# Two Fourier heads on one core: x of the second head in rotating tiles, its stores without an order among themselves, six compare buffers and a narrower rank-one product

## The chip, the cores and the metric

The kernel runs on one core of a Trainium2 chip. The time is that of one execution in device microseconds, lower is better; the figure is the median of several executions. A profile is one further execution, recorded by the hardware profiler.

## What is computed

Two independent heads, each on a tensor of 2048 rows by 512 columns in float32, written side by side. Head A is a global filter (a 2D real FFT, a product with a complex weight, the inverse). Head B is FNet mixing: two DFT matrices come in as inputs, and the real part of the double transform goes out.

```python
def _A_ref(x, w_r, w_i):
    X = jnp.fft.rfft2(x, axes=(-2, -1))
    return jnp.fft.irfft2(X * (w_r + 1j * w_i), s=(S, D), axes=(-2, -1))

def _B_ref(x, dft_seq_re, dft_seq_im, dft_hid_re, dft_hid_im):
    a = jnp.einsum("bsd,ed->bse", x, dft_hid_re)
    b = jnp.einsum("bsd,ed->bse", x, dft_hid_im)
    return jnp.einsum("ts,bse->bte", dft_seq_re, a) - jnp.einsum("ts,bse->bte", dft_seq_im, b)

return jnp.concatenate([A, B], axis=-1)
```

## The kernel before

The kernel does not multiply by B's matrices. It computes both heads by fast transforms with its own small tables, and beside that it reads B's matrices completely (36 MB) and checks that they are the DFT matrices which the fast way assumes. The sum of all differences gives a flag; if it is not small, a slow general way (`_b_from_c`) runs after the branch. With the usual inputs only the branch is paid. So three streams of work share the engines:

*The compare stream* (`compare`, `compare_hidden`). 64 pieces of 512 KB of the sequence matrices and 4 of the hidden ones are loaded by SP to buffers named `raw` (three, the constant RAW), VectorE (DVE) forms the difference with a table piece `tt` (lines L309 and L311), and ScalarE (ACT) sums the absolute values of two pieces at once (L302). The pieces come in a fixed order; C_AT pins each to a step of A's work, so that it is not done before it.

*Head A* (`a_work`). `forward` loads x of A to `zv`, adds and subtracts halves on DVE, and for eight pairs of groups does the transform along the hidden dimension (L455, 128x256, into PSUM, copied by ACT L489), then the first step along the sequence (L455, 128x512, copied by L496). POOL stores the result to `out_a` as a bounce buffer (16 stores, L498), and SP loads it back in another layout to `zv` (eight loads, L510). Eight slots follow (`slot`): DVE sums (L226), a product with the `ft` table, the weight product on DVE, sums on DVE, two-column corrections on POOL (L581, L582), a product with the `it` table, and a copy back into `zv` by ACT (L600). When all eight are done, `inverse` runs 256 products on TensorE (PE) in two halves (from `zv`, then from `sda`) with copies by ACT (L619, L630), and SP stores `out_a` (L634).

*Head B* (`b_work`). `b_load` brings x of B to a region `big` by eight loads of 512 KB and one small one, and POOL copies its middle column (L373). Each load fills 64 partitions: a half of the partitions holds four groups of rows, the other half the mirrored rows in reverse. Four folds on DVE (`b_fold`, even part to a `yb` tile, odd part in place), 64 products along the sequence (`b_along`, L397, copied by ACT L401 to L403), nine steps along the hidden dimension (`b_hidden`, L410 to L415; L412 is a rank-one product of one row with 257 columns of a table that is zero in every second one), and eight output row groups (`b_rows`): a product (L422 and its kin), a copy to a row buffer `yb` (L429; two buffers, YB), two sums on DVE, a mirrored copy (L432), a direct store (L440, L442) and an indirect one that scatters the mirrored rows (L443), both on POOL's queue. All these stores write the tensor `out_b`, and the framework orders each behind the ones before it.

What sets the order: B_AT names the step of A after which each step of B is issued, C_AT pins the compares; a scheduler of the framework then places the instructions of every engine in one fixed sequence and puts in the semaphore waits. An engine, POOL's and SP's queues too, works strictly in that sequence: an instruction that waits holds up all behind it. Each DMA also waits for the DMA issued eight before it on its queue, since eight semaphores go round.

Of the kernel before, what the change touches and what calls it, by code (L numbers as in the profile page):

```python
# [10 lines left out]
F32 = mybir.dt.float32  # L11
# [55 lines left out]
def _tables_b():  # L67
# [133 lines left out]
def kernel(  # L201
# [43 lines left out]
    def region(name):  # L245

        return ap.tile([P, 8208 if name == "big" else 8192], F32, name=name)
# [12 lines left out]
    hc = bp.tile([P, 2, 257], F32, name="hc")  # L260
# [101 lines left out]
    def b_load():  # L362

        xt = region("big")
        x = xt.rearrange("p (g d) -> p g d", g=16)
        src = xb.rearrange("b a d -> (b a) d")
# [7 lines left out]
        nc.gpsimd.dma_start(fb, tabs["fb"].rearrange("p k (j s) -> p k j s", j=8))  # L374
        nc.sync.dma_start(hc, tabs["hc"])
        hidden_table()
        nc.sync.dma_start(mb, tabs["mb"])
        return x

    def b_fold(q, x):  # L380

        v = x[:, 4 * q : 4 * q + 4]
        ev = bp.tile([P, 2, 512], F32, name="yb", bufs=YB).rearrange("p k (g d) -> p (k g) d", g=2)
        TT(out=ev, in0=v[:, :, :256], in1=v[:, :, 512:256:-1], op=ADD)
        TT(out=v[:, :, :256], in0=v[:, :, :256], in1=v[:, :, 512:256:-1], op=SUB)
# [19 lines left out]
    def b_hidden(e, zb):  # L405
# [4 lines left out]
        nc.tensor.matmul(out, ye[:, :, 0, at[0]], hc[:, 0], start=True, stop=False)  # L410
        nc.tensor.matmul(out, ye[:, :, 1, at[0]], ht[:, 1, 0], start=False, stop=False)
        nc.tensor.matmul(out, yo[0:1, :, at[1]], hc[0:1, 1], start=False, stop=True)  # L412
        for c in range(2):
            nc.tensor.matmul(bank[:, 257:], yo[:, :, at[2] + 16 * c], ht[:, c, 1, 1:256], start=c == 0, stop=c == 1)  # L414
        nc.scalar.copy(zb[:, e], bank)  # L415

    def b_rows(o, zb):
# [16 lines left out]
        if o == 0:  # L434
            bank = ps_b.tile([P, 512], F32, name="pb")
            nc.tensor.matmul(bank[0:1, :257], mb[:, 1408:], zb[:, 0, :257], start=True, stop=True)
            nc.scalar.copy(y[0:1, 1, :257], bank[0:1, :257])
            nc.scalar.copy(y[0:1, 1, 257:], y[0:1, 1, 255:0:-1])
            for k in range(2):
                nc.gpsimd.dma_start(rows[8 * k, :64], y[64 * k : 64 * k + 64, 0])  # L440
        else:
            nc.gpsimd.dma_start(rows[o], y[:, 0])  # L442
# [389 lines left out]
```

## Time and profile before

| | us |
|---|---|
| median of 3 runs | 277.77 |
| lowest, highest | 274.91, 278.9 |
| the profiled execution | 278.1 |
| its span, first to last instruction | 276.3 |

| engine | busy us | share of the span |
|---|---|---|
| PE (matmuls) | 211.5 | 77% |
| DVE | 161.2 | 58% |
| ACT | 136.0 | 49% |
| POOL | 42.8 | 15% |

The DMA engines moved 73.85 MB at a mean of 267 GB/s. No engine is busy throughout, so the shares alone do not say what sets the time; it has to be read stage by stage. In the rows of the profile, "out<-in" names the tiles written and read, "xN" is a count, and the bracket at the end gives the idle time ahead of an instruction on its engine and what ended it. "SPq" and "POOLq" are the engines as issuers of DMAs. A row of the waits reads: engine and line, what it waited for, us in total, how often, the longest. "PEclk" is the share of full clock that TensorE was granted. A row of 128x256 or so of PE often counts each product as two matmul records.

### The profile page before, as it was taken

The numbers are of one execution on the slowest core, as the hardware profiler recorded it, in microseconds if no ns is written. First come the engines' busy times: TensorE is split into PE (matmuls) and PEld (weight loads), VectorE is DVE, ScalarE is ACT, GpSimd is POOL, SyncE is SP. The second block draws the span as 40 slices with busy tenths as digits, with TensorE's granted clock in tenths as the row PEclk, the third lists the DMA queues.
The fourth block names the chain that finished last, engine by engine and source line by source line (L and its number), as shares of the span: only waits on it lengthen the run. The fifth ranks groups of instructions, "written<-read, shape, count | busy, mean of one in ns | idle before, by whom it ended". The sixth has DMA issues, their size and how long they took to land.

```text
span 276.3 us, 2713 instructions
## 1 busy us (share of the span) xinstructions
PE 211.5 (77%) x833; PEld 169.0 (61%) x833; DVE 161.2 (58%) x225; ACT 136.0 (49%) x219; POOL 42.8 (15%) x80
## 2 busy tenths in 40 slices
PE   5049999299878799999999676302999995999630
PEld 1039788177678358787875445002799994876520
DVE  0860001685748359797968679745485754675340
ACT  1001430649866251856337235415678775774570
POOL 3000120013210016250213333013010100000000
PEclk9658999899955599999999797755599999899795
DMA  7999999889995998585844343775979888889763
GB/s 256 403 243 214 215 379 418 293 267 343 354 401 181 367 399 311 193 248 194 289 145 109 141 161 103 288 250 208 284 250 332 298 259 294 273 279 369 287 264 126
DMA packets 27460, 73.85 MB, mean 267 GB/s; under 512 B 2928, under 2 KB 9072, under 8 KB 26928
## 3 DMA queue, kind: packets, MB, share of 16 engines
q1 hardware_dynamic: 24432, 64.48, 70.5%
q0 software_dynamic: 2720, 8.56, 8.2%
q10 hardware_dynamic: 288, 0.59, 0.7%
q8 instruction: 8, 0.13, 0.2%
q14 instruction: 12, 0.10, 0.1%
HBM read 61.03 MB, written 12.58 MB: 266 GB/s over the span
## 4 chain that ended last, share of the span: by engine, by line
DMA 48%; PE 24%; DVE 13%; issue 8%; ACT 4%; SPq 1%; POOL 0%; DVEq 0%; POOLq 0%; ACTq 0%
DMA raw<-in_cm 23%; PE pa L455 12%; DMA ht<-tab_ht 6%; DMA out_b<-yb,turn 6%; DMA big<-in_xb 6%; DVE ec L309 5%; PE pb L414 4%; DVE ec L311 3%; PE pb L412 3%; DMA zv<-in_xa 2%; DMA zv<-out_a 2%; ACT ec L302 2%; DMA out_b<-yb 2%; DVE yb L226 2%; DVE sda L226 2%
## 5 line engine op out<-in xcount | busy, mean ns | idle before, releaser
L302 ACT ACTIVATE ec<-ec 128x2048 bf16<-128x2048 bf16 x34 | 65.0, 1911 | 33.4 <-DVE ec L311 21.8
L311 DVE TENSOR_TENSOR ec<-raw,tt 128x512 bf16<-128x512 f32 (+1 forms) x48 | 40.0, 865 | 51.7 <-DMA raw<-in_cm 51.6
L309 DVE SCALAR_TENSOR_TENSOR ec<-tt,odd,raw 128x512 bf16<-128x512 f32 (+1 forms) x48 | 42.5, 926 | 19.2 <-DMA raw<-in_cm 18.9
L455 PE MATMUL pa<-zb,sda 128*128 128x256 f32 x128 | 32.2, 410 | 12.2 <-DVE sda L226 12.2
L455 PEld LDWEIGHTS pa<-zb,sda 128*128 128x128 f32 x128 | 30.4, 307 | 15.5 <-DVE sda L226 13.1
L455 PE MATMUL pa<-ye,sda 128*128 128x256 f32 x128 | 32.2, 414 | 6.5 <-ACT zb L630 3.4
L455 PEld LDWEIGHTS pa<-ye,sda 128*128 128x128 f32 x128 | 26.4, 208 | 12.2 <-ACT zb L630 4.6
L455 PE MATMUL pa<-it,sda 128*128 128x128 f32 x112 | 19.2, 339 | 17.9 <-POOL sda L581 16.0
L455 PEld LDWEIGHTS pa<-it,sda 128*128 128x128 f32 x112 | 17.9, 246 | 23.6 <-POOL sda L581 20.1
L455 PE MATMUL pa<-ye,zv 128*128 128x256 f32 x128 | 30.5, 403 | 0.7 <-ACT zv L600 0.7
L455 PEld LDWEIGHTS pa<-ye,zv 128*128 128x128 f32 x128 | 29.3, 306 | 1.8 <-ACT zv L600 1.0
L226 DVE TENSOR_TENSOR sda<-zv 128x512 f32<-128x512 f32 x30 | 19.5, 687 | 15.4 <-DMA zv<-in_xa 7.5
L226 DVE TENSOR_TENSOR sda<-sda 128x512 f32<-128x512 f32 (+1 forms) x34 | 23.0, 717 | 0.3
L489 ACT COPY zb<-pa 128x1024 f32<-128x1024 f32 x8 | 8.1, 1007 | 28.5 <-PE pa L455 28.5
L226 DVE TENSOR_TENSOR sda<-pa,sda 128x1024 f32<-128x1024 f32 (+1 forms) x16 | 17.7, 1151 | 5.6 <-ACT sda L557 3.9
L455 PE MATMUL pa<-zb 128*128 128x512 f32 x32 | 16.6, 645 | 5.5 <-ACT zb L489 5.5
L397 PE MATMUL pb<-fb,yb 128*128 128x72 f32 x64 | 14.5, 319 | 3.1 <-ACT ye L403 3.1
L397 PEld LDWEIGHTS pb<-fb,yb 128*128 128x128 f32 x64 | 13.1, 248 | 6.2 <-ACT ye L403 4.0
L397 PE MATMUL pb<-fb,big 128*128 128x128 f32 (+1 forms) x64 | 16.5, 351 | 0.0
L498 POOL DMA_DIRECT2D out_a<-zb x16 | 8.5, 534 | 49.5 <-ACT zb L496 49.3
L429 ACT COPY yb<-pb 128x514 f32<-128x514 f32 x8 | 4.7, 587 | 19.4 <-DMA out_b<-yb,turn 17.1
L397 PEld LDWEIGHTS pb<-fb,big 128*128 128x128 f32 x64 | 13.1, 251 | 1.0 <-issue 1.0
(78 smaller groups left out, 247.0 us busy)
## 6 DMA issues: line engine op xcount, KB each, us to landing
raw<-in_cm SPq DMA_DIRECT2D x64, 512.0 KB, 4.9
tt<-tab_tt SPq DMA_DIRECT2D x8, 513.0 KB, 10.3
zv<-in_xa SPq DMA_DIRECT2D x8, 512.0 KB, 8.6
big<-in_xb SPq DMA_DIRECT2D x8, 512.0 KB, 16.1
out_a<-zb POOLq DMA_DIRECT2D x16, 256.0 KB, 6.2
sda<-in_wa SPq DMA_DIRECT2D x16, 256.0 KB, 3.4
zv<-out_a SPq DMA_DIRECT2D x8, 512.0 KB, 8.7
out_a<-zb SPq DMA_DIRECT2D x4, 1024.0 KB, 6.9
```

What stands on the lines that cost most here:

```text
L226: last[0] = nc.vector.tensor_tensor(**kw)
L302: nc.scalar.activation(flat, flat, mybir.ActivationFunctionType.Abs, accum_out=stat[:, i : i + 1])
L309: nc.vector.scalar_tensor_tensor(out, v, odd[:, k : k + 1], raw, op0=MUL, op1=SUB)
L311: nc.vector.tensor_tensor(out=out, in0=raw, in1=v, op=ADD if flip else SUB)
L397: nc.tensor.matmul(bank[:, at : at + n].rearrange("p (j s) -> p j s", j=8), v[:, cols], f[:, :, k], start=True, stop=True)
L412: nc.tensor.matmul(out, yo[0:1, :, at[1]], hc[0:1, 1], start=False, stop=True)
L414: nc.tensor.matmul(bank[:, 257:], yo[:, :, at[2] + 16 * c], ht[:, c, 1, 1:256], start=c == 0, stop=c == 1)
L429: nc.scalar.copy(y[:, :, :257], bank[:, :257].unsqueeze(1).to_broadcast([P, 2, 257]))
L455: mma[0] = nc.tensor.matmul(*args, **kw)
L489: nc.scalar.copy(zs[p], pd[p])
L498: nc.gpsimd.dma_start(bounce[:, 2 * p + k], ys[:, k])
```

## The change

It has five parts and new numbers in both tables.

- x of B is loaded to tiles `xq` (two, of 128 partitions by four groups), each by four loads of 256 KB to all 128 partitions (partition 2r holds row r of a group, partition 2r+1 its mirror); the first two quarters at the start, the third and fourth after the first and second have been used. The table `fb` is permuted to match. POOL's copy of the middle column is gone: each fold is now two instructions of 4 x 255 columns and two of 4 columns instead of two of 1024. The region `big` is gone, and the nine results of `b_hidden` lie in the two `xq` buffers and a tile of their own.
- The stores of `out_b` are declared independent of each other.
- RAW is 6 instead of 3.
- The rank-one product reads a tile of ones and writes 128 columns, every second one of the output; the table `hc` loses its second half.
- B_AT and C_AT are new.

```diff
-RAW = 3
-B_AT = [4, 10, 10, 12, 12, 14, 14, 14, 14, 15, ..., 26, 28, 30, 32, 35, 38, 40, 42]
+RAW = 6
+B_AT = [2, 6, 6, 8, 8, 8, 8, 8, 8, 8, 8, 8, 11, 12, 17, 19, 19, 19, 19, 26, 28, 30, 32, 35, 38, 38, 42]
...
-        for q in range(4):
-            g = slice(4 * q, 4 * q + 4)
-            for half, lo in enumerate((1 + 16 * q, 112 - 16 * q)):
-                v = src[16 * lo : 16 * lo + 256].rearrange("(g r) d -> r g d", g=4)
-                load(x[64 * half : 64 * half + 64, g, :512], v[:, ::-1] if half else v)
-        load(x[64:80, 15, :512], src[:16])
-        nc.gpsimd.tensor_copy(x[:, :, 512], x[:, :, 256])
...
+    def b_load(q):
+        x = bp.tile([P, 4, 512], F32, name="xq", bufs=2)
+        for k in range(4):
+            g = 4 * q + k
+            lo, hi = 1 + 4 * g, 124 - 4 * g
+            load(x[:, k], bass.AP(xb.tensor, xb.offset + 16 * D * lo, [[D, 64], [16 * D * (hi - lo), 2], [1, D]]))
+        if q == 3:
+            load(x[1:32:2, 3], xb[0])
+        return x
...
-        TT(out=ev, in0=v[:, :, :256], in1=v[:, :, 512:256:-1], op=ADD)
-        TT(out=v[:, :, :256], in0=v[:, :, :256], in1=v[:, :, 512:256:-1], op=SUB)
+        for out, op in ((ev, ADD), (x, SUB)):
+            TT(out=out[:, :, 1:256], in0=x[:, :, 1:256], in1=x[:, :, 511:256:-1], op=op)
+            TT(out=out[:, :, 0], in0=x[:, :, 0], in1=x[:, :, 256], op=op)
...
-        nc.tensor.matmul(out, yo[0:1, :, at[1]], hc[0:1, 1], start=False, stop=True)
+        nc.tensor.matmul(bank[:, 1:257:2], yo[0:1, :, at[1]], ones[0:1], start=False, stop=True)
...
+        for st in stores:
+            tc.declare_no_dep(st.ins, group="rows", reason="each store has rows of its own")
+            tc.add_to_no_dep_group("rows", st.ins)
...
     def b_work():
-        x = b_load()
+        x = {0: b_load(0)}
+        yield
+        x[1] = b_load(1)
+        nc.gpsimd.dma_start(fb, tabs["fb"].rearrange("p k (j s) -> p k j s", j=8))
         yield
         for q in range(4):
-            ev = b_fold(q, x)
+            ev = b_fold(x[q])
             yield
             for g in range(4 * q, 4 * q + 4):
-                b_along(g, x, ev)
+                b_along(g, x[q], ev)
+            if q < 2:
+                x[q + 2] = b_load(q + 2)
```

The lines of the changed kernel are shifted: L443 becomes L434, L442 L433, L581 and L582 L576 and L577, L323 L322, L510 L505, L309 and L311 L308 and L310, L226 L225.

The order of instructions moves in three places. The first is POOL's queue among B's output rows; `DMASWk` is the k-th of the eight semaphores of its DMAs, so that a wait on the number just ahead is a wait for the store issued last. Before:

```order
L443 DMA out_b<-yb,turn 2048x512 [waits DMASW5_49,DMASW6_49,DMASW4_49,Activation_49]
L520 COPY sda<-we 128x2x2 [waits DMAHW5_49,DVE_49]
L581 COPY sda<-sda 128x2 [waits DVE_49,Pool_49]
L442 DMA out_b<-yb 128x512 [waits DMASW7_49,DMASW6_49,Activation_49]
L582 TENSOR_TENSOR sda<-sda,sg 128x2 [waits DVE_49,Pool_49]
L443 DMA out_b<-yb,turn 2048x512 [waits DMASW7_49,DMASW0_49]
L442 DMA out_b<-yb 128x512 [waits DMASW1_49,DMASW0_49,Activation_49]
L520 COPY sda<-we 128x2x2 [waits DMAHW0_49,DVE_49,Pool_49]
L581 COPY sda<-sda 128x2 [waits DVE_49,PE_49,Pool_49]
L582 TENSOR_TENSOR sda<-sda,sg 128x2 [waits DVE_49,PE_49,Pool_49]
L443 DMA out_b<-yb,turn 2048x512 [waits DMASW2_49,DMASW1_49]
```

Now:

```order
L434 DMA out_b<-yb,turn 2048x512 [waits DMASW6_49,Activation_49]
L433 DMA out_b<-yb 128x512 [waits DMASW7_49,Activation_49]
L434 DMA out_b<-yb,turn 2048x512 [waits DMASW0_49,DVE_49]
L515 COPY sda<-we 128x2x2 [waits DMAHW4_49,Pool_49]
L526 COPY sda<-zv 128x2 [waits DMAHW1_49,DVE_49,Pool_49]
L527 TENSOR_TENSOR sda<-zv,sg 128x2 [waits Pool_49]
L576 COPY sda<-sda 128x2 [waits DVE_49]
L577 TENSOR_TENSOR sda<-sda,sg 128x2 [waits DVE_49]
L433 DMA out_b<-yb 128x512 [waits DMASW1_49,Activation_49]
L434 DMA out_b<-yb,turn 2048x512 [waits DMASW2_49,DVE_49]
L433 DMA out_b<-yb 128x512 [waits DMASW3_49,Activation_49]
L434 DMA out_b<-yb,turn 2048x512 [waits DMASW4_49,DVE_49]
```

Every store before waits for the store right ahead of it and for the one eight issues back; now only the second is left, and two rows' stores can stand in one piece of the queue.

The second is SP's queue between the first compares and the load that brings A's bounced rows back (`zv<-out_a`). Before:

```order
L281 DMA big<-in_xb 16x512
L287 DMA ft<-tab_fwd 128x128
L287 DMA i_382<-tab_inv 128x512
L287 DMA ft<-tab_fwd 128x128
L287 DMA it<-tab_inv 128x128 x2
L323 DMA raw<-in_cm 128x1024 x9
L287 DMA sda<-in_wa 128x2x256 x2
L287 DMA sda<-tab_fwd 128x512
L287 DMA sda<-in_wa 128x2x256 x2
L323 DMA raw<-in_cm 128x1024 x5
L510 DMA zv<-out_a 128x2x512 x8
```

Now:

```order
L322 DMA raw<-in_cm 128x1024 x5
L295 DMA tt<-tab_tt 128x1026
L322 DMA raw<-in_cm 128x1024 x9
L280 DMA xq<-in_xb 128x1x512 x4
L322 DMA raw<-in_cm 128x1024 x5
L280 DMA xq<-in_xb 128x1x512 x4
L280 DMA xq<-in_xb 16x512
L286 DMA sda<-in_wa 128x2x256 x2
L286 DMA sda<-tab_fwd 128x512
L286 DMA sda<-in_wa 128x2x256
L505 DMA zv<-out_a 128x2x512 x8
```

The second half of x of B (`xq`) stands between compare loads, the small tables of the slots behind `zv<-out_a`; in all 20 compare loads instead of 17 are issued ahead of it. On PE, 40 of B's 64 products along the sequence stand ahead of A's last 128x512 pair of the forward part instead of 11, and 8 instead of 12 behind the first products of slot 0.

The third is DVE's end of A's slots (`sda` are A's sums, `yb<-yb,pb` are B's rows, `ec<-raw` the compares). Before:

```order
L309 SCALAR_TENSOR_TENSOR ec<-tt,odd,raw 128x512 x6
L226 TENSOR_TENSOR sda<-pa,sda 128x1024 x2
L226 TENSOR_TENSOR yb<-yb,pb 128x255 x2
L311 TENSOR_TENSOR ec<-raw,tt 128x512 x4
L226 TENSOR_TENSOR sda<-sda 128x512 x2
L311 TENSOR_TENSOR ec<-raw,ht 128x514
L311 TENSOR_TENSOR ec<-raw,ht 128x510
L226 TENSOR_TENSOR yb<-yb,pb 128x255 x2
L226 TENSOR_TENSOR sda<-sda 128x512 x2
L311 TENSOR_TENSOR ec<-raw,ht 128x258
```

Now:

```order
L225 TENSOR_TENSOR sda<-sda 128x512 x4
L225 TENSOR_TENSOR yb<-yb,pb 128x255 x2
L225 TENSOR_TENSOR sda<-pa,sda 128x1024 x2
L225 TENSOR_TENSOR yb<-yb,pb 128x255 x2
L225 TENSOR_TENSOR sda<-sda 128x512 x4
L225 TENSOR_TENSOR sda<-pa,sda 128x1024 x2
L225 TENSOR_TENSOR sda<-sda 128x512 x4
L308 SCALAR_TENSOR_TENSOR ec<-tt,odd,raw 128x512 x6
L310 TENSOR_TENSOR ec<-raw,tt 128x512 x4
L310 TENSOR_TENSOR ec<-raw,ht 128x514
```

Five compares of the sequence matrices stood among the last slots' sums; now all of B's rows and A's sums come first, and 41 compares behind them. B's last row is now ahead of the sums of the last two slots; before, it came behind all of them, after the compares with the hidden table.

More of the change, by code (lines that the diff above doesn't have):

```diff
@@ L245, in region @@
     def region(name):
-        return ap.tile([P, 8208 if name == "big" else 8192], F32, name=name)
+        return ap.tile([P, 8192], F32, name=name)
     def part(v, kb, *shape):
@@ L409, in b_hidden @@
         out = bank[:, :257]
-        nc.tensor.matmul(out, ye[:, :, 0, at[0]], hc[:, 0], start=True, stop=False)
+        nc.tensor.matmul(out, ye[:, :, 0, at[0]], hc, start=True, stop=False)
         nc.tensor.matmul(out, ye[:, :, 1, at[0]], ht[:, 1, 0], start=False, stop=False)
-        nc.tensor.matmul(out, yo[0:1, :, at[1]], hc[0:1, 1], start=False, stop=True)
+        nc.tensor.matmul(bank[:, 1:257:2], yo[0:1, :, at[1]], ones[0:1], start=False, stop=True)
         for c in range(2):
             nc.tensor.matmul(bank[:, 257:], yo[:, :, at[2] + 16 * c], ht[:, c, 1, 1:256], start=c == 0, stop=c == 1)
-        nc.scalar.copy(zb[:, e], bank)
+        nc.scalar.copy(zb[e], bank)
     def b_rows(o, zb):
@@ L435, in b_rows @@
             bank = ps_b.tile([P, 512], F32, name="pb")
-            nc.tensor.matmul(bank[0:1, :257], mb[:, 1408:], zb[:, 0, :257], start=True, stop=True)
+            nc.tensor.matmul(bank[0:1, :257], mb[:, 1408:], zb[0][:, :257], start=True, stop=True)
             nc.scalar.copy(y[0:1, 1, :257], bank[0:1, :257])
             nc.scalar.copy(y[0:1, 1, 257:], y[0:1, 1, 255:0:-1])
-            for k in range(2):
-                nc.gpsimd.dma_start(rows[8 * k, :64], y[64 * k : 64 * k + 64, 0])
-        else:
-            nc.gpsimd.dma_start(rows[o], y[:, 0])
-        nc.gpsimd.indirect_dma_start(
+            stores = [nc.gpsimd.dma_start(rows[8 * k, :64], y[64 * k : 64 * k + 64, 0]) for k in range(2)]
+        else:
+            stores = [nc.gpsimd.dma_start(rows[o], y[:, 0])]
+        stores.append(nc.gpsimd.indirect_dma_start(
             out=out_b, out_offset=bass.IndirectOffsetOnAxis(ap=turn[:, o : o + 1], axis=0),
-            in_=y[:, 1], in_offset=None)
+            in_=y[:, 1], in_offset=None))
+        for st in stores:
+            tc.declare_no_dep(st.ins, group="rows", reason="each store has rows of its own")
+            tc.add_to_no_dep_group("rows", st.ins)
     signs = ap.tile([P, 5], F32, name="sg")
@@ L666, in b_work @@
     def b_work():
-        x = b_load()
+        x = {0: b_load(0)}
+        yield
+        x[1] = b_load(1)
+        nc.gpsimd.dma_start(fb, tabs["fb"].rearrange("p k (j s) -> p k j s", j=8))
         yield
         for q in range(4):
-            ev = b_fold(q, x)
+            ev = b_fold(x[q])
             yield
             for g in range(4 * q, 4 * q + 4):
-                b_along(g, x, ev)
+                b_along(g, x[q], ev)
+            if q < 2:
+                x[q + 2] = b_load(q + 2)
+            if q == 2:
+                nc.sync.dma_start(hc, tabs["hc"])
+                hidden_table()
+                nc.sync.dma_start(mb, tabs["mb"])
             yield
-        zb = part(region("big"), 0, 9, 512)
+        za, zc = (bp.tile([P, 4, 512], F32, name="xq", bufs=2) for _ in range(2))
+        zb = [z[:, k] for z in (za, zc) for k in range(4)] + [bp.tile([P, 512], F32, name="z8")]
         for e in range(9):
@@ L692 @@
     b_at, c_at = list(B_AT), list(C_AT)
+    while b_at and b_at[0] < 0:
+        b_at.pop(0)
+        next(b)
     for n in range(100):
```

33 lines of the change are left out of this document (11 added, 22 removed).

## The prediction

> **What bounds the kernel now.** I read the views in this order: busy time by stretches of the span, then who waited for whom, then the order of time around the longest waits. The stretches are cut where A's work changes: until the first load of A's half-transformed rows lands (92.3), until B's first output row is read from PSUM (142.7), until A's inverse starts (195.9), until its last matmul (264.6), and the end.
>
> ```profile
> core 0: us, PE busy (x) PEld busy (x) DVE busy (x) ACT busy (x) POOL busy (x), PEclk, DMA share, GB/s
> 0.00:92.30 92.30, 68.78 (x273) 55.42 (x273) 41.65 (x59) 39.35 (x74) 11.71 (x27) 0.83 0.94 306
> 92.30:142.70 50.40, 49.69 (x179) 37.18 (x180) 38.74 (x50) 22.77 (x46) 14.03 (x21) 0.95 0.79 272
> 142.70:195.90 53.20, 29.95 (x125) 20.28 (x124) 38.60 (x65) 23.50 (x39) 13.83 (x29) 0.75 0.55 178
> 195.90:264.60 68.70, 62.19 (x256) 55.60 (x256) 40.60 (x48) 46.04 (x56) 3.19 (x4) 0.92 0.86 295
> 264.60:276.30 11.70, 0.93 (x4) 0.50 (x2) 1.64 (x4) 4.38 (x5) 0.00 (x0) 0.66 0.46 186
> ```
>
> Each stage has another limit. The first fills the DMA engines (share 0.94). The second is PE's: 49.69 of 50.40 us busy. The third is nobody's: PE 29.95 of 53.20, DMA 0.55, so something waits. The fourth is PE's again (62.19 of 68.70), with a busy DMA beside it. The waits name the third stage:
>
> ```profile
> POOL out_b L442 <- DMA out_b<-yb,turn: 22.0, 4, 7.9
> PEld pa L455 <- POOL sda L581: 20.1, 4, 12.8
> POOL out_b L443 <- DMA out_b<-yb: 18.2, 6, 5.2
> ACT yb L429 <- DMA out_b<-yb,turn: 17.1, 5, 8.1
> PE pa L455 <- POOL sda L581: 16.0, 4, 11.2
> ```
>
> POOL waits 40 us in all until one store of B has landed before it issues the next. PE waits 16 us for two-column copies of POOL (L581). In order of time one sees that these are the same wait:
>
> ```profile
> 180.37 1.00 POOL L443 DMA_INDIRECT out_b<-yb,turn  x1 [2.96 <-DMA out_b<-yb]
> ...
> 189.22 0.56 POOL L442 DMA_DIRECT2D out_b<-yb  x1 [7.86 <-DMA out_b<-yb,turn]
> 190.90 0.49 POOL L581 COPY sda<-sda 128x2 f32<-128x2 f32 x1 [1.12 <-DVE sda L226]
> 191.44 3.78 PE L455 MATMUL pa<-it,sda 128*128 128x128 f32 x16 [11.20 <-POOL sda L581]
> 195.90 1.65 PE L455 MATMUL pa<-ye,zv 128*128 128x256 f32 x3 [0.68 <-ACT zv L600]
> ```
>
> The row buffer of B's next row is free only when the scatter of 180.37 has landed (8 us), its copies and sums follow, DVE's part of A's last slot stands behind them, POOL's copy behind that, and PE and the whole inverse (195.90) behind the copy.
>
> **The change part by part, and the sum.** Times are of the profiled execution: span 276.3, execution 278.1, so 1.8 lies around the span. The median of the runs (277.77) is 0.3 lower.
>
> *x of B, and the first stage.* The old loads write 64 partitions each; the rate falls by half while they run. A load of the same 2 KB pieces to 128 partitions, zv from out_a, does not show that:
>
> ```profile
> GB/s 373 402 407 412 417 397 412 417 402 345 181 201 206 238 204 211 226 214 211 228 204 211 233 201 206 236 199 221 226 206 214 228 199 207 252 413 426 417 433 400
> ...
> big<-in_xb SPq DMA_DIRECT2D x8, 512.0 KB, 16.1
> ...
> GB/s 236 440 210 251 297 348 379 333 328 261 323 358 369 394 369 404 405 394 410 394 405 405 404 379 399 389 389 384 399 374 415 374 426 395 436 379 430 410 420 420
> ```
>
> The first row is us 7 to 40 in slices of 0.8 us, 25 of them near 215; the last is us 88 to 104, with the zv loads in its first half. So 4.2 MB take 20 us, and at 400 they would take 10. Half of x now comes at once (2.1 MB, 5 us instead of 20), and B's fold and the first compare start some 15 us earlier. What the end gets of it is less, since A's path sets the stage:
>
> ```profile
> 53.75 3.39 PE L455 MATMUL pa<-zb 128*128 128x512 f32 x4 [5.48 <-ACT zb L489]
> ...
> 72.29 14.37 SPq L323 DMA_DIRECT2D raw<-in_cm  x5
> ...
> 86.97 5.95 SPq L510 DMA_DIRECT2D zv<-out_a  x8
> ...
> 75.55 1.06 POOL L498 DMA_DIRECT2D out_a<-zb  x2 [0.19 <-issue]
> ...
> out_a<-zb POOLq DMA_DIRECT2D x12, 256.0 KB, 5.9
> ...
> 98.64 1.51 PE pb L397 x14
> ```
>
> The last bounce stores are issued at 75.55 to 76.6 and land 5.9 later, at 82.5. The load of zv is issued at 86.97, because it stands on SP behind five compare loads that wait for buffers. With six buffers that wait is over sooner, but now 40 instead of 11 of B's products along the sequence stand on PE ahead of A's last ones: 29 of two records at 1.51/14 = 0.108, so 6.3 us. The 5.48 us in which PE waited for ACT (ACT sat behind its first compare) go, since the compares are earlier. So the last store moves by +0.8 and the zv load goes out near 83.4: -3.5, of which I take **-3**. Bounds: -9 (if all 10 us of DMA time counted) and +4 (if ACT's wait stays: 6.3 instead of 0.8 on 83.4 less 87.0, and 2 for the last quarter of x, which SP issues only once the second quarter is used up). The small parts: eight more x loads on SP (0.7 us each by 5.95/8 of the row above, in time when SP would wait for buffers anyway), eight more DVE instructions of four columns a row, and POOL's copy of the middle column and its wait gone. DVE is busy 41.65 of 92.3 here, which hides them; without that cover they are 2 us.
>
> *The rank-one product of 128 columns, and the second stage.* PE is the limit, so its instructions count in full.
>
> ```profile
> 104.92 0.78 PE pb L412 x2
> ...
> 163.55 2.05 PE L455 MATMUL pa<-it,sda 128*128 128x128 f32 x16 [1.75 <-POOL sda L581]
> ```
>
> 257 columns cost 0.78 a product, 128 columns 2.05/8 = 0.26. Nine times 0.52 is 4.7 us. The new product writes every second column, which no matmul of this trace does. The bounds are 0 (no gain) and 4.7, and a write with a stride could even lose; I take 4.7, since the number of columns is what sets the cost in all rows here. The Trainium skill speaks against it: "SBUF — State Buffer", in the note on cache lines of the section on Door 1, says that PSUM has lines of two fp32 values and that any non-contiguous PSUM pattern slows matmuls significantly. By that rule the 4.7 would be lost, and the sum below would be 4.7 higher; no run here shows it.
>
> Four more along products have moved ahead (0.9 us), and one group of eight `it` products of slot 1 (2.05) stands behind B's first row now. 50.4 - 4.7 - 0.9 - 2.0 = 42.8. DVE has the same ten compares and slot work (38.74) in this stage and would be 90% busy, so I take **45**. Bounds 42.8 and 50.4.
>
> *Stores not ordered, and the third stage.* Each store now waits only for the eighth store before it. POOL's 40 us of waits go; what is late next is the row buffer (two of them), which still waits until both stores of its old row have landed:
>
> ```profile
> 154.63 0.59 ACT L429 COPY yb<-pb 128x514 f32<-128x514 f32 x1 [3.35 <-DMA out_b<-yb,turn]
> ...
> 161.08 0.59 ACT L429 COPY yb<-pb 128x514 f32<-128x514 f32 x1 [0.74 <-DMA out_b<-yb,turn]
> 161.70 0.75 DVE L226 TENSOR_TENSOR yb<-yb,pb 128x255 f32<-128x255 f32 x2 [0.77 <-ACT yb L429]
> 163.68 2.35 DVE L226 TENSOR_TENSOR sda<-pa,sda 128x1024 f32<-128x1024 f32 x2 [1.23 <-POOL sda L582]
> 164.12 0.60 ACT L432 COPY yb<-yb 128x510 f32<-128x510 f32 x1
> 165.64 1.07 ACT L600 COPY zv<-pa 128x512 f32<-128x512 f32 x2 [0.92 <-PE pa L455]
> 166.07 2.69 DVE L226 TENSOR_TENSOR sda<-sda 128x512 f32<-128x512 f32 x4
> ...
> L443 POOL DMA_INDIRECT out_b<-yb,turn x8: 998/1039/1597, 151.7 to 215.2; - x8
> L442 POOL DMA_DIRECT2D out_b<-yb x7: 558/560/595, 155.1 to 209.4; - x7
> ...
> out_b<-yb,turn POOLq DMA_INDIRECT x6, 4.0
> ```
>
> One turn of a buffer is 0.59 + 0.75 + 0.60 + 0.56 + 1.04 + 4.0 = 7.5 us, with 1 us for other work in the queues 8.5 for two rows, 4.3 a row (before: 6.45 between 154.63 and 161.08). Seven intervals are 30; row 0's two extra copies and its extra store, each at most 0.60, 1.3. DVE's new order has ten sums of A's last two slots behind row 7: 0.59 + 0.75, then 2.69 + 2.35 + 2.69, POOL 0.49, PE's last eight products 2.05, ACT 1.07: 12.7. Together **44** instead of 53.2. Bounds: PE's own 29.95 + 2.05 = 32, and 53.2.
>
> *Six compare buffers, and the fourth stage.*
>
> ```profile
> DVE ec L311 <- DMA raw<-in_cm: 51.6, 19, 27.3
> ...
> 196.00:266.40 70.40, 41.27 (x48) 0.92 0.83 287
> ...
> raw<-in_cm SPq DMA_DIRECT2D x32, 512.0 KB, 4.8
> ```
>
> 32 compares took 70.4 us with 41.27 of DVE work: with three buffers each load's 4.8 us is a wait. Now 41 compares stand behind A's last slot instead of being fitted in between, 6 of them loaded by then. 35 loads (18.3 MB), two tables, half of out_a and B's last rows are 22.5 MB: 76 us at the stage's 295 GB/s, 56 at the 400 of a full queue. From 174 (4 before the inverse) that ends between 230 and 250; PE's chain ends at 178 + 62 to 69. I take PE's chain at **66**: of the 6.5 us in which it waited for ACT, which sat behind late compares, some goes. Bounds 62 and 75. A rule of the Trainium skill would help here: "TensorE: Matmul & The Clock Gate", section on HAM oscillation, has the clock halved after some 3.4 us of idle time. The trace agrees (0.75 in the stage with the 11.2 us gap); a shorter gap would save at most 0.08 x 68.7 = 5.5, which I leave out of the sum. The end stays 11.7: last compares, flag, branch.
>
> Sum: 92.3 - 3 = 89.3; + 45 = 134.3; + 44 = 178.3; + 66 = 244.3; + 11.7 = 256.0; + 1.8 = 257.8, so **258 us**, -7%.
>
> **The rivals.** *The rows keep their pace.* DVE's order now has B's row 7 ahead of the last two slots' sums, before only row 6. So a slow row costs more than before: the inverse starts at 134.3 + 7 x pace + 14.0, and the time is 79.5 later. At the old 6.45 us that is 273, no change; at 8 us, the landing of the scatter at 180.37, it is **284**, slower; at 7.2 nothing is gained, and from 7.9 on it is slower by 2%. For it: the buffers are still two. Against it: the 8 us came with compare loads beside the scatter; with six buffers full few loads run there, and six scatters of this stage landed in 4.0.
>
> *DMA sets the tail.* If six loads in flight move no more than 295 GB/s, the last compare is loaded at 250, and with 11 for its DVE and ACT work and the end the time is 263. Against it: three in flight already reach a share of 0.86 with pauses.
>
> *PE sets the third stage.* If the rows hold nothing, it takes 32 to 35 instead of 44: 246 to 249, and 242 with the fourth at its 62 too. Against it: the two row buffers.
>
> *The strided product is no cheaper.* Then 0.78 stays nine times: 263. Against it: all rows here go by columns; for it: none of them writes with a stride.
>
> *The first stage gains nothing or loses.* +4 instead of -3 gives 265.
>
> **How the numbers follow.** My forecast (250 to 263 with its own bounds, the tail by DMA included) gets 0.45; the product at its old price 0.10; PE as the limit, 242 to 250, 0.15; rows at 5 to 6.4 us or a lost first stage, 263 to 272, 0.17; rows at the old pace, 272 to 283, 0.08; slower rows 0.05. Faster by over 2% (below 272.2; 2% is what a measurement here can tell) is 0.87, the same 0.08, slower 0.05. The range 246 to 272 leaves out 0.13 above and about 0.06 below.
>
> **What would show it.** Right: PE's wait for POOL's copy (L576 now) under 4 us, the inverse near 178, rows 4 to 5 us apart, the rank-one product at 0.26, first compare near 31, zv loaded near 89. Wrong: ACT's wait for the row buffers still over 15 us (rows), a zv load after 95 (first stage), or DVE's wait for compare loads still over 30 us after the inverse starts (tail).

## The result, and the profile after

| | before | after |
|---|---|---|
| median, us | 278.33 (4 runs beside it) | 244.31 (4 runs) |
| lowest to highest | 274.91 to 279.71 | 242.67 to 245.61 |
| ratio, 95% interval | | 0.8811, 0.8704 to 0.8918 |
| profiled execution, span | 278.1, 276.3 | 244.79, 243.0 |

Faster by 12%, where 7% was forecast, and 1.7 us below the range. The profiled executions of four runs below (stores ordered, stores free in the kernel before, 64 partitions, 257 columns) lie at the slow end of their times, so their rows are used for what waits on what, and the medians for sizes. Differences between kernels in us are of medians taken on four chips, on which the kernel before had medians of 276.9 to 278.3; by the ratios to it, the differences of the first set below come out 3 to 4 us larger. The stretches of the profile after are cut at the same five events as in the prediction (zv back 81.9, B's first output row 129.1, inverse 170.2, PE's last matmul of A 230.9, end):

```profile
core 0: us, PE busy (x) PEld busy (x) DVE busy (x) ACT busy (x) POOL busy (x), PEclk, DMA share, GB/s
0.00:81.90 81.90, 62.58 (x281) 50.95 (x281) 42.54 (x67) 40.05 (x76) 12.42 (x26) 0.96 0.93 351
81.90:129.10 47.20, 46.51 (x167) 35.77 (x168) 34.03 (x44) 22.03 (x43) 9.72 (x17) 0.93 0.84 297
129.10:170.20 41.10, 28.61 (x129) 18.93 (x127) 37.30 (x58) 19.63 (x36) 18.57 (x37) 0.92 0.53 176
170.20:230.90 60.70, 58.05 (x256) 53.52 (x256) 46.67 (x63) 52.09 (x62) 0.00 (x0) 0.97 0.95 364
230.90:243.00 12.10, 0.58 (x2) 0.50 (x2) 1.26 (x4) 2.57 (x4) 0.00 (x0) 0.56 0.34 137
```

| stage | before | forecast | after | after less forecast |
|---|---|---|---|---|
| 1, to zv | 92.3 | 89.3 | 81.9 | -7.4 |
| 2, PE | 50.4 | 45 | 47.2 | +2.2 |
| 3, rows of B | 53.2 | 44 | 41.1 | -2.9 |
| 4, inverse | 68.7 | 66 | 60.7 | -5.3 |
| 5, end | 11.7 | 11.7 | 12.1 | +0.4 |
| span | 276.3 | 256.0 | 243.0 | -13.0 |

Of the gain of 33.3 us, 10.4 came in stage 1, 3.2 in 2, 12.1 in 3 and 8.0 in 4. Stage 3 is now DVE's (37.30 of 41.10), and in stage 4 PE (58.05 of 60.70) and the DMA engines (share 0.95) are both nearly full. The waits that named stage 3 before have shrunk, and POOL's two waits for a store (22.0 and 18.2 us) are no longer among them:

```profile
PE pa L450 <- POOL sda L576: 9.8, 4, 4.2
POOL out_b L433 <- ACT yb L424: 8.9, 7, 2.0
DVE ec L310 <- DMA raw<-in_cm: 6.0, 4, 3.4
DVE ec L308 <- DMA raw<-in_cm: 5.8, 5, 4.1
ACT yb L421 <- DMA out_b<-yb,turn: 4.5, 4, 2.2
```

ACT waited 17.1 us for the row buffers before. L310 waited 51.6 for compare loads (as L311), but only 1.6 of that in stage 3: 27.3 were the wait for the first compare, and in stage 4 the two compare lines waited 28.9. B's rows, in ACT's copies of them (the view of one line: duration, first and last start), are (156.0 - 129.1)/7 = 3.8 us apart; the forecast was 4.3:

```profile
L421 ACT COPY yb<-pb x8: 590/591/608, 129.1 to 156.0; 128x514 f32<-128x514 f32 x8
```

In stage 1 the rate of the DMA engines while x of B comes is the first thing to read: us 7 to 40 in slices of 0.8 us, where before 25 slices stood near 215.

```profile
GB/s 376 402 397 417 402 417 412 412 402 385 392 387 387 385 387 382 404 405 411 425 410 408 407 408 403 417 412 407 407 417 397 422 403 427 383 412 427 417 407 407
DMA packets 4334, 13.36 MB, mean 405 GB/s; under 512 B 518, under 2 KB 646, under 8 KB 4333
```

Then the path to zv, PE's last 128x512 pair, ACT's copy, POOL's store and SP's load. Before, these four stood at 70.29, 73.29, 75.55 and 86.97. First three rows of the timeline after, then the load by its line:

```profile
68.31 1.93 PE L450 MATMUL pa<-zb 128*128 128x512 f32 x4
70.31 1.01 ACT L491 COPY zb<-pa 128x1024 f32<-128x1024 f32 x1 [1.24 <-issue]
71.62 1.05 POOL L493 DMA_DIRECT2D out_a<-zb  x2 [2.49 <-ACT zb L491]
```

```profile
L505 SPq DMA_DIRECT2D zv<-out_a x8: 380/464/559, 78.2 to 82.0; - x8
```

The store goes out 3.9 us earlier, the load 8.8 earlier, and zv is used 10.4 earlier. Two rows of the timeline of before show what else held the store there: ACT did a compare's sum (1.91) ahead of the last copy, and ahead of the store POOL's copy L520 waited until 75.02 for a load of A's weight:

```profile
70.96 1.91 ACT L302 ACTIVATE ec<-ec 128x2048 bf16<-128x2048 bf16 x1 [0.23 <-DVE ec L311]
...
75.02 0.34 POOL L520 COPY sda<-we 128x4 f32<-128x4 f32 x1 [3.41 <-DMA sda<-in_wa]
```

### The profile page after: what moved, and what is told of

It is laid out like the page before. It is cut to its first block, busy times and chain, and to the rows that moved or that the text cites. A ratio compares the mean times of both kernels' runs of the same rounds, so it can differ in the third digit from the quotient of the medians.

```text
span 243.0 us, 2736 instructions
## 1 busy us (share of the span) xinstructions
PE 196.3 (81%) x833; PEld 159.7 (66%) x833; DVE 161.8 (67%) x233; ACT 136.4 (56%) x219; POOL 40.7 (17%) x79
## 4 chain that ended last, share of the span: by engine, by line
PE 56%; DMA 14%; DVE 12%; issue 6%; ACT 5%; POOL 3%; SPq 0%; POOLq 0%; DVEq 0%; ACTq 0%
PE pa L450 41%; DVE sda L225 10%; DMA raw<-in_cm 4%; PE pb L406 4%; PE pb L389 4%; ACT ec L301 3%; DMA zv<-in_xa 3%; DMA out_a<-zb 2%; PE pb L404 2%; PE pb L402 2%; PE pb L403 2%; DMA zv<-out_a 2%; DMA sda<-in_wa 1%; DMA out_b<-yb,turn 1%; DVE ec L310 1%
## 5 line engine op out<-in xcount | busy, mean ns | idle before, releaser
L308 DVE SCALAR_TENSOR_TENSOR ec<-tt,odd,raw 128x512 bf16<-128x512 f32 (+1 forms) x48 | 42.1, 926 | 11.5 <-DMA raw<-in_cm 5.8
L310 DVE TENSOR_TENSOR ec<-raw,tt 128x512 bf16<-128x512 f32 (+1 forms) x48 | 39.1, 866 | 13.8 <-DMA raw<-in_cm 6.0
L225 DVE TENSOR_TENSOR sda<-zv 128x512 f32<-128x512 f32 x30 | 19.4, 686 | 19.0 <-PE pa L450 7.0
L450 PE MATMUL pa<-ye,sda 128*128 128x256 f32 x128 | 27.8, 379 | 0.0
L450 PEld LDWEIGHTS pa<-ye,sda 128*128 128x128 f32 x128 | 24.3, 190 | 3.3
L450 PE MATMUL pa<-it,sda 128*128 128x128 f32 x112 | 17.0, 311 | 10.6 <-POOL sda L576 9.8
L450 PEld LDWEIGHTS pa<-it,sda 128*128 128x128 f32 x112 | 15.8, 220 | 14.0 <-POOL sda L576 11.8
L225 DVE TENSOR_TENSOR sda<-sda 128x512 f32<-128x512 f32 (+1 forms) x34 | 23.1, 721 | 1.6 <-ACT sda L561 1.3
L225 DVE TENSOR_TENSOR sda<-pa,sda 128x1024 f32<-128x1024 f32 (+1 forms) x16 | 17.8, 1153 | 3.4 <-ACT sda L552 1.8
L225 DVE TENSOR_TENSOR yb<-xq 128x1020 f32<-128x1020 f32 (+1 forms) x8 | 5.2, 690 | 17.7 <-DMA xq<-in_xb 17.6
L450 PE MATMUL pa<-zb 128*128 128x512 f32 x32 | 15.2, 598 | 0.0
L595 ACT COPY zv<-pa 128x512 f32<-128x512 f32 x16 | 8.6, 589 | 11.6 <-PE pa L450 11.6
L389 PE MATMUL pb<-fb,xq 128*128 128x128 f32 (+1 forms) x64 | 13.6, 299 | 0.6 <-DVE xq L225 0.6
L450 PE MATMUL pa<-sda,ft 128*128 128x512 f32 x28 | 13.3, 596 | 0.0
L389 PEld LDWEIGHTS pb<-fb,yb 128*128 128x128 f32 x64 | 10.5, 200 | 3.9 <-issue 3.6
## 6 DMA issues: line engine op xcount, KB each, us to landing
xq<-in_xb SPq DMA_DIRECT2D x16, 256.0 KB, 7.0
out_a<-zb POOLq DMA_DIRECT2D x16, 256.0 KB, 5.8
sda<-in_wa SPq DMA_DIRECT2D x16, 256.0 KB, 3.8
```

Source lines behind the costliest of these rows:

```text
L225: last[0] = nc.vector.tensor_tensor(**kw)
L308: nc.vector.scalar_tensor_tensor(out, v, odd[:, k : k + 1], raw, op0=MUL, op1=SUB)
L310: nc.vector.tensor_tensor(out=out, in0=raw, in1=v, op=ADD if flip else SUB)
L389: nc.tensor.matmul(bank[:, at : at + n].rearrange("p (j s) -> p j s", j=8), v[:, cols], f[:, :, k], start=True, stop=True)
L450: mma[0] = nc.tensor.matmul(*args, **kw)
L595: nc.scalar.copy(out[:, :, 32 * h : 32 * h + 32].rearrange("p x (q g) -> p q x g", q=2), pi[:, h].rearrange("p q (x g) -> p q x g", x=16))
```

## The experiments

Twelve kernels ran, in three sets. Theory 1 in the expectations is that of the prediction: several parts, each worth its term. Every ratio is to the kernel before, timed on the same chip.

### One part undone, or done alone

**Stores ordered again**, the rest as changed:

```diff
-        for st in stores:
-            tc.declare_no_dep(st.ins, group="rows", reason="each store has rows of its own")
-            tc.add_to_no_dep_group("rows", st.ins)
```

> The changed kernel with the stores of B ordered again. Theory 1 (the order among the stores held POOL's queue and with it the row buffers): the waits of POOL for stores come back at 30 us or more, rows stand 6 to 7 us apart instead of 3.8, and since B's last row now stands ahead of the last two slots the inverse starts at 129 + 7 x 6.5 + 14 = 188 instead of 170: about 262 us. Rival (the two row buffers wait for the same landings anyway, and the gain of the third stage came from the new order of work): no more than 4 us, 244 to 248.

Measured 252.94 us, ratio 0.9224 (0.9089 to 0.9358): 8.6 more. The waits of POOL for the store before are back, ACT waits 11.7 us instead of 4.5 for a row buffer, and the inverse starts at 177.7 instead of 170.2:

```profile
POOL out_b L434 <- DMA out_b<-yb: 19.7, 7, 6.1
...
ACT yb L421 <- DMA out_b<-yb,turn: 11.7, 6, 3.9
```

The order is worth about 9 us here (11 by the ratios), between the two theories. The rows are 6.5 us apart, as theory 1 had it (128.8 to 174.2 for the eight copies), but the inverse starts 3.5 us after the last of them begins and not 14: without the free stores the scheduler also put A's last sums ahead of B's last row.

**The same freedom alone in the kernel before:**

```diff
+        for st in stores:
+            tc.declare_no_dep(st.ins, group="rows", reason="each store has rows of its own")
+            tc.add_to_no_dep_group("rows", st.ins)
```

> The kernel before with the stores of B not ordered, nothing else. Theory 1: POOL's 40 us of waits for stores go, the inverse starts some 10 us earlier than 195.9, the fourth stage is as long as before: 264 to 270 us. Rival (without the other parts the row buffers or the compares hold the third stage): 275 to 280.

Measured 277.63 us, ratio 1.0066 (0.9963 to 1.0169): nothing that can be told from noise. B's rows do come sooner (copies from 145.6 to 183.8, before from 142.7 to 198.1), but the inverse starts at 200.0. DVE's waits for compare loads, 47.2 us in the whole run, are not the reason: 2.2 us of them fall between 140 and 200. In the third stage DVE is busy 44.28 of 54.40 us, and the compares alone (second row, tile `ec`) take 17.65 there, 27 of them; before, 22 took 11.81:

```profile
145.60:200.00 54.40, 30.50 (x125) 20.18 (x124) 44.28 (x72) 28.30 (x45) 20.20 (x33) 0.72 0.73 250
145.60:200.00 54.40, 0.00 (x0) 0.00 (x0) 17.65 (x27) 12.03 (x12) 0.72 0.73 250
```

The time that the stores give up is filled with compares, which with the old due times stand between the sums of A's last slots. Stages 3 and 4 together take 122.4 us, 121.9 before.

**Three compare buffers** in the changed kernel:

```diff
-RAW = 6
+RAW = 3
```

> The changed kernel with three compare buffers. Theory 1 (in the last stage three loads in flight left the DMA engines pauses, and ACT's copies for PE stood behind late compares): the fourth stage goes back from 60.7 to about 68 us, its rate from 364 to about 295 GB/s, and the first stage gives back part of its 10 us, since SP is held by the compare loads ahead of the load of zv: 252 to 258 us. Rival (the shorter load of x made the room, buffers matter little): 244 to 248.

Measured 278.85 us, ratio 1.0208 (1.0119 to 1.0296). Both forecasts were wrong: the whole gain is lost, 34.5 us. Theory 1 was right on the fourth stage (68 us and 295 GB/s forecast) and did not see that the end gets 13.9 us longer. Its stretches 4 and 5, cut at its own events:

```profile
179.40:249.00 69.60, 59.25 (x256) 53.31 (x256) 39.76 (x50) 45.75 (x54) 0.00 (x0) 0.98 0.83 286
249.00:275.00 26.00, 0.58 (x2) 0.50 (x2) 9.89 (x17) 9.71 (x12) 0.00 (x0) 0.59 0.56 202
```

And of its waits the last one of PE, for the flag of the compares:

```profile
PE pb L718 <- DVE rs L716: 19.9, 1, 19.9
```

With three loads in flight stage 4 moves 286 GB/s (295 before) against 364 with six. PE has done the inverse by 249 and then waits 19.9 us for the compare stream, which now ends last (5.9 in the changed kernel).

**x of B in loads of 64 partitions**, 2 KB pieces as before:

```diff
-            load(x[:, k], bass.AP(xb.tensor, xb.offset + 16 * D * lo, [[D, 64], [16 * D * (hi - lo), 2], [1, D]]))
+            for s in range(2):
+                load(x[64 * s : 64 * s + 64, k],
+                     bass.AP(xb.tensor, xb.offset + 16 * D * lo + 32 * D * s, [[D, 32], [16 * D * (hi - lo), 2], [1, D]]))
```

> The changed kernel with each load of x split in two that write 64 partitions each (128 KB each, 2 KB a piece as now). Theory 1 (64 partitions take half the rate): while x loads, the rate falls from 405 to about 215 GB/s, so the first half of x takes 10 us instead of 5 and the second half the same, and the first stage gets 3 to 8 us longer: 247 to 252 us. Rival (the old rate came from the reversed order of rows or the four strided groups of one load): the rate stays near 400 and the time within 2 us of 244.

Measured 248.36 us, ratio 0.905 (0.8934 to 0.9166): 4 more, as theory 1 had it. The same window as above:

```profile
GB/s 366 392 412 407 397 422 417 407 410 323 211 268 271 236 253 229 241 209 209 194 321 314 253 255 295 332 345 331 373 313 254 293 378 432 422 397 412 422 407 422
DMA packets 3805, 10.93 MB, mean 331 GB/s; under 512 B 582, under 2 KB 710, under 8 KB 3804
```

2.4 MB less arrive by 40 us, and A's bounce stores follow: the last is issued at 74.89 instead of 71.62. These loads are half as large as well (128 KB), but that is not the reason for the low rate: the 512 KB loads to 64 partitions of the kernel before ran near 215.

### Buffers and tables of due times

The run with three buffers left open whether three buffers or an order made for six lost the gain. Two tables by two numbers of buffers, with x, stores and product as changed in all four:

```diff
-B_AT = [2, 6, 6, 8, 8, 8, 8, 8, 8, 8, 8, 8, 11, 12, 17, ..., 35, 38, 38, 42]
-C_AT = [..., 0, 8, 8, 8, 8, 10, 10, 10, 10, 18, 18, 18, 18, 18, 34, ..., 34, 40, ..., 40]
+B_AT = [4, 4, 10, 10, 12, 12, 14, 14, 14, 14, 15, 15, 15, 15, 17, ..., 35, 38, 40, 42]
+C_AT = [..., 0, 6, 6, 6, 6, 6, 35, ..., 35, 37, ..., 37]
```

> The changed kernel with six buffers, but with the two tables of due times of before (B's with its first entries 4, 4, 10, 10, one entry more at the start for the second piece of x). Theory (the six buffers carry the gain, the tables only use them): 244 to 250 us, and the third stage longer by the compares that stand between B's rows. Rival (the gain is the order's, the compares out of the third stage): 256 us or more.

> As the run with the old tables of due times, but with three compare buffers: x in rotating tiles to 128 partitions, the free stores and the narrow rank-one product alone. Theory (with three buffers it was the tail of 41 compares behind the last slot that lost everything, so an order with fewer compares there keeps what x and the stores give): 262 to 270 us. Rival (with three buffers nothing is gained whatever the order, since the stream of compares ends last): 274 to 280.

> The changed kernel with four compare buffers (three gave 278.9 us, six 244.3). Theory (the tail of compares turns at a buffer's load and work divided by the buffers, 2.2 us with three, and PE is the limit again at about 1.5): four give 1.65 to 1.8 us a compare and 250 to 262 us. Rival (a threshold: four already feed it): 244 to 248.

| buffers | tables of before | new tables |
|---|---|---|
| 3 | 269.03 (0.9698, 0.9609 to 0.9787) | 278.85 |
| 4 | | 257.13 (0.9269, 0.9167 to 0.9371) |
| 6 | 257.44 (0.9291, 0.9196 to 0.9386) | 244.31 |

Neither column nor row has one price. x, stores and product alone (269.03) are worth some 9 us. Six buffers add 11.6 with the old tables and 34.5 with the new; the new tables cost 9.8 with three buffers and gain 13.1 with six. For the old tables with six buffers the rival had the time right (257.44), for three buffers the theory (269.03), and four buffers are in between, as the theory of that run had it. Why the old tables lose with six is in the stretches of that run, cut at its own events:

```profile
0.00:91.40 91.40, 61.67 (x276) 50.24 (x277) 55.07 (x80) 48.34 (x81) 11.28 (x26) 0.91 1.01 391
91.40:143.90 52.50, 52.50 (x198) 40.49 (x198) 32.28 (x44) 15.46 (x43) 5.47 (x24) 0.93 0.45 157
143.90:188.10 44.20, 24.69 (x104) 16.57 (x102) 40.16 (x66) 26.36 (x41) 18.39 (x27) 0.77 0.74 268
188.10:244.50 56.40, 56.37 (x258) 52.79 (x258) 33.42 (x45) 45.21 (x55) 2.18 (x2) 1.00 0.75 280
```

Its compares crowd stage 1 (DVE 55.07 there against 42.54, DMA full), zv is back only at 91.4, and after that the DMA engines are no longer full (0.45 to 0.75). The rival's reason, compares in the third stage, is the smaller part: that stage is 3.1 us longer than in the changed kernel, the first two together 14.8, and the rest is 6.5 shorter. The new tables leave more of the compares to stage 4, where PE is busy anyway; six buffers can stream them there, three cannot. With four buffers PE still waits 14.2 us at the end for the compares. That the crowded first stage delays zv is read from these rows; no run changes it alone.

### The rank-one product

**257 columns again:**

```diff
-        nc.tensor.matmul(bank[:, 1:257:2], yo[0:1, :, at[1]], ones[0:1], start=False, stop=True)
+        nc.tensor.matmul(out, yo[0:1, :, at[1]], hc[0:1, 1], start=False, stop=True)
```

> The changed kernel with the rank-one product over 257 columns again (and its table of two columns of rows). The trace of the changed kernel has 0.67 us for two products of the line (0.335 each in the chain, 0.455 mean), where the prediction had 0.26. Theory (the product's time is set by loading its weights, taken from a tile in which they lie 25 elements apart): the second stage gets 0.1 to 0.2 us a product longer, 1 to 2 us, so 245 to 247 us. Rival (the columns count in full, as predicted, and something else ate the gain): 9 x 0.52 = 4.7 more, 249 us.

**128 adjoining columns**, and **weights from the row of ones**, one edit each:

```diff
-        nc.tensor.matmul(bank[:, 1:257:2], yo[0:1, :, at[1]], ones[0:1], ...)
+        nc.tensor.matmul(bank[:, 1:129], yo[0:1, :, at[1]], ones[0:1], ...)
...
+        nc.tensor.matmul(bank[:, 1:257:2], ones[0:1], ones[0:1], ...)
```

> The changed kernel, but the rank-one product is added to columns 1 to 128 of the bank instead of every second column of 1 to 256, so that the rank-one terms land in the wrong columns of B. If a write with a stride is what keeps the product at 0.455 us mean, it falls to near 0.26. If its weights set it, it stays within 0.03 of 0.455 and the time within 1% of 244.

> The changed kernel, but the rank-one product takes its weights from the row of ones, which lies contiguous, instead of the row of yo with 25 elements from one to the next, so that B's rank-one term is left out (a constant is added in its place). If the weights set the product, its weight load falls from 319 ns to about 190 and the product below 0.40 mean. If the strided write sets it, the product stays at 0.455 within 0.03.

**All hidden products' weights dense**, and that with 257 columns:

```diff
-    ye = bp.tile([P, 2304], F32, name="ye").rearrange("p (j c s) -> p j c s", c=2, s=9)
-    yo = bp.tile([P, 128, 25], F32, name="yo")
+    ye = bp.tile([P, 2304], F32, name="ye").rearrange("p (c s j) -> p j c s", c=2, s=9)
+    yo = bp.tile([P, 25, 128], F32, name="yo").rearrange("p s j -> p j s")
```

> The changed kernel with the same instructions, but ye and yo laid out so that the 128 weights of each hidden product lie next to each other (they were 18 and 25 elements apart). Theory (the second stage of 47.2 us, in which PE is busy 46.5, is held by weight loads of 312 to 330 ns where contiguous ones take 190): five loads a step, nine steps, up to 0.13 us each, so 3 to 6 us less there, 238 to 241 us in all. Rival (weight loads hide beside the products; and the copies that write ye and yo get no dearer): 243 to 246. If the copies of PSUM into ye and yo get dearer by the new stride of their output, up to 250.

> Dense weights of the hidden products (238.3 us with the narrow product) with the rank-one product over 257 columns. Theory (once the weights load in 182 to 190 ns, the columns set the price): two records of the product take 0.60 us, as the other products of 257 columns with dense weights, instead of 0.48; 239 to 241 us. Rival (the price is that of an instruction, not of columns): 0.48 to 0.52 and no difference.

The rows of the weight load and the product (lowest, median and highest ns). As changed:

```profile
L404 PEld LDWEIGHTS pb<-ones,yo x18: 307/319/333, 91.0 to 123.8; 1*128 1x128 f32 x18
L404 PE MATMUL pb<-ones,yo x18: 397/462/600, 91.0 to 123.9; 1*128 1x128 f32 x18
```

128 adjoining columns:

```profile
L404 PE MATMUL pb<-ones,yo x18: 397/448/500, 92.2 to 123.8; 1*128 1x128 f32 x18
```

Weights from the row of ones:

```profile
L404 PEld LDWEIGHTS pb<-ones x18: 181/182/184, 92.1 to 121.4; 1*128 1x128 f32 x18
L404 PE MATMUL pb<-ones x18: 270/321/372, 92.1 to 121.5; 1*128 1x128 f32 x18
```

Dense weights:

```profile
L404 PE MATMUL pb<-ones,yo x18: 270/321/372, 90.2 to 117.7; 1*128 1x128 f32 x18
```

Dense weights with 257 columns:

```profile
L405 PE MATMUL pb<-hc,yo x18: 375/427/479, 91.7 to 124.7; 1*128 1x257 f32 x18
```

As the weights lie, the stride of the output does next to nothing (462 to 448); the stride of the weights sets the price: 319 ns to load 128 weights that lie 25 elements apart, 182 for adjoining ones, and the product falls with it. No run has dense weights and adjoining columns, so what the gaps cost there is open. A pair of records is one product. The prediction's 0.78 is such a pair in the chain of the work that ended last; on the timeline, where a record overlaps the next, it was 0.84 before. In the changed kernel the chain has 0.67, which the expectation of the run with 257 columns took for two products, and the timeline:

```profile
102.55 0.74 PE L404 MATMUL pb<-ones,yo 1*128 1x128 f32 x2
```

With 257 columns:

```profile
101.90 0.84 PE L405 MATMUL pb<-hc,yo 1*128 1x257 f32 x2
```

With dense weights:

```profile
98.92 0.48 PE L404 MATMUL pb<-ones,yo 1*128 1x128 f32 x2
```

With both:

```profile
101.06 0.70 PE L405 MATMUL pb<-hc,yo 1*128 1x257 f32 x2
```

So the narrower product gains 0.10 each as the weights lie, 0.22 with dense ones. It never reaches 0.26, and one thing stays open: with dense weights the rank-one product of 257 columns takes 0.63 in the chain of its run, and the product of 257 columns ahead of it 0.43. As the weights lie, nine times 0.10 is 0.9 us, and in the whole time it can't be seen: 243.67 us with 257 columns, ratio 0.8744 (0.8669 to 0.8819), against 244.31. The theory named for that run (1 to 2 us) was too high. The kernels with 128 adjoining columns and with weights from the row of ones, which leave B's rank-one term in the wrong columns or out, ran once each, in 241.94 and 242.08 us, just under the changed kernel's lowest (242.67), and dense weights with 257 columns 245.16; single times, which tell nothing of 2 us.

Dense weights in the whole kernel: **238.33 us**, ratio 0.8621 (0.8554 to 0.8688), faster than both kernels, and than the run with 257 columns on the same chip by 3 to 5 us (ratios 0.8621 and 0.8744; all six of its times lie below all six there). From one hidden step to the next right behind it PE takes 2.34 us instead of 2.82 (95.62 to 97.96 and 98.72 to 101.54 on the timelines), nine times 0.48 is 4.3 of the 5.7 by which the second stage is shorter. In the chain about half of a step's gain is the rank-one product's (0.67 to 0.41), most of the rest that of the two products of L406 (1.26 to 1.06). B's first row is at 122.6 instead of 129.1, the inverse at 165.8 instead of 170.2. ACT's three copies that write these weights got dearer, as the expectation feared (medians 384, 338 and 462 ns instead of 272, 234 and 300, some 6 us in all), and the gain is what remains after that.

## Why the prediction was right, and where it failed

The forecast of 258 us was 14 too high, and 244.31 lies below its range of 246 to 272. The step that failed by most is the path to zv in stage 1, then the size of stage 4 and what limits stage 3; the price of the rank-one product failed the other way.

*The first stage, -3: the largest miss (-7.4).* The gain of 10.4 lies beyond even the prediction's own bound of 9. The rate with 128 partitions (400, measured 405) and the first compare at 27.3 were right or better. The step that failed is "So the last store moves by +0.8 and the zv load goes out near 83.4". The store moved by -3.9, 4.7 off. PE had 45 records more in the stretch up to the end of A's last pair (201 from 27 to 70.2 us, 156 from 27 to 72.2 before), where the step counted 58, and was busy only 3.48 us more, not 6.3. The stretch after, and that of before:

```profile
27.00:70.20 43.20, 43.20 (x201) 35.68 (x200) 20.46 (x24) 31.25 (x58) 7.43 (x14) 1.00 0.97 376
```

```profile
27.00:72.20 45.20, 39.72 (x156) 31.20 (x155) 17.64 (x17) 23.41 (x29) 7.61 (x15) 0.96 0.97 322
```

Of the 2.8 that are missing, the granted clock of 1.00 against 0.96 is an estimated 1.6 to 1.7, and nine of B's records, which PE had done before us 27, are another 1.0 at the step's 0.108 each. All 5.48 of its idle time went, as the step had it. ACT's compare and POOL's copy ahead of the store, which the sum left out, were another 2. Behind the store the wait on SP fell by 4.9 us (11.4 to 6.55), near the 4.3 of the step, and the reload, which the sum took as unchanged, by 1.6. Loads to 128 partitions are 4 us of the total by the run with 64 (6.6 by the ratios).

*The rank-one product, 4.7: failed.* The choice that failed is "the number of columns is what sets the cost in all rows here". The rows compared (0.78 and 0.26) differed in more than columns: the weights of the first are one row whose elements lie 25 apart, those of the second 128 rows of adjoining ones. The term was 0.9, near the bound of none, and the rival of the product that gets no cheaper (chance 0.10) was right as to this term. The rule of the Trainium skill set against the step ("SBUF — State Buffer", the section on Door 1), that a PSUM output with gaps slows a matmul, was not the reason either; by the run with adjoining columns the gaps cost 0.014 us in the median as the weights lie. The same note of the Trainium skill also gives SBUF lines of 16 bytes and a penalty for an access that leaves its line at each element. With that half the runs agree: 319 against 182 ns. With 0.9 in place of 4.7 the terms of stage 2 give 50.4 - 0.9 - 0.9 - 2.0 = 46.6, and 47.2 was measured.

*Stores and rows, 44: 2.9 too long, with another limit.* That POOL's waits for stores go was right. The step that failed is that the row buffers are late next: ACT waited 4.5 us for them in all, and DVE was busy 37.30 of the 41.10. Seven intervals took 26.9, where 30 and 1.3 for row 0 were reckoned, and the part behind the last row 14.2 instead of 12.7. One sign was wrong: PE's wait for POOL's copy is 9.8 us, not under 4. It no longer stands for a store: of the four copies' waits POOL's own for DVE's sums are 19.1 us. The rival of rows at the old pace fell; stores that wait cost some 9 here. Its pace of 6.45 was one interval: the eight copies before lay from 142.7 to 198.1, 7.9 apart in the mean, and by its own formula that gives 283 us, not 273. That free stores gain by themselves was implied by adding terms, and alone they gain nothing.

*The fourth stage, 66: mis-sized by 5.3.* PE's chain did set it, as forecast. PE's busy time fell by 4.1 (62.19 to 58.05, clock 0.92 to 0.97), which the sum named and left out, and its idle time from 6.5 to 2.65, of which the sum credited 2.7 of 3.9. Six buffers moved 364 GB/s, between the 295 and the 400 of the prediction's two ends. What sets the clock stays open. It was 1.00 in the run with old tables and six buffers, where PE hardly waited (56.37 busy of 56.40), and 0.92 before, where it waited 6.5; but 0.98 with three buffers, where it waited 10.4 (69.60 - 59.25). So the rule on the clock gate that the prediction took from the Trainium skill ("TensorE: Matmul & The Clock Gate", section on HAM oscillation) is neither shown nor refuted in this stage.

*The conceptual miss.* The prediction priced the buffers as a shortening of waits inside the fourth stage, and the rival "DMA sets the tail" at 263 with six. It did not ask what the new order would be without them. The runs show that buffers and tables are one change: 278.85 + 257.44 - 269.03 - 244.31 = 23 us of the gain need both. A tail set by the compare stream, as in "DMA sets the tail", is what happens with three and four buffers (PE waits 19.9 and 14.2 us for it at the end), not with six (5.9).

*The chances.* The direction was right; the stages add up to 13.0 us less than the sum, 2.2 more in the second and 15.6 less in the first, third and fourth. The rival "PE sets the third stage", 246 to 249 or 242, came nearest in time and was wrong in mechanism: DVE, not PE, is busy 37.30 of the 41.10.

## What to carry to other kernels

A term for a deeper buffer pool and a term for a new order must not be added: ask for each what it is worth without the other, and where the work goes that the order moves, since here the same table costs 10 us with three buffers and gains 13 with six. Price a small matmul by its weight load as well as by its columns; lay out the stationary operand so that its elements adjoin, and let the copy that writes it, which had time to spare, take the stride. When following a path to its end, list what stands ahead of each step on every queue it crosses: ACT and POOL held the last store here, and for it the prediction looked only at PE.

## What the runs showed of the hardware

- While x of B came in 2 KB pieces to 128 partitions, 256 KB a load, the DMA engines moved a mean of 405 GB/s (us 7 to 40 of the changed kernel). While it came to 64 partitions they moved 194 to 271 (eleven slices of the run with 64) and near 215 (25 slices of the kernel before).
- A weight load of 128 columns of fp32 took 182 to 190 ns in the median with adjoining elements (run with dense weights) and 303 to 335 with 16, 18, 25 or 64 elements from one to the next (changed kernel). Adjoining ones took as long (333) in a stretch of the run with dense weights whose granted clock was 0.53. What the stride adds to a product differs: in the chain a pair of records of 257 columns took 0.46 us instead of 0.43, two pairs of 255 columns 1.26 instead of 1.06, the rank-one pair of 128 columns 0.67 instead of 0.41.
- An output in PSUM with every second fp32 column cost 14 ns of 462 while the weights were strided; with dense weights no run compares it.
